# Row statistics and router logits made per segment inside the recurrent chain, instead of in one pass over x in the first step

## The chip, the core and the metric

The kernel runs on one core of a Trainium2 chip. A core has a matrix engine (TensorE, PE in the profile; its weight loads are listed as PEld), a vector engine (VectorE, DVE), an activation engine (ScalarE, ACT), GpSimd (POOL) and SyncE (SP), which here only issues DMAs. Each engine runs its own instructions in order and waits on semaphores for the others. SP, POOL and ACT all issue DMAs, and 16 DMA engines of the core carry them out. SBUF holds working data; PSUM holds what PE writes.

The metric is the device time of one execution in microseconds, lower is better. A run is one such execution; the profile is of one more.

## The reference

Two results are added to x. A is a recurrent transformer layer with memory: x is normalised per row and cut into 64 segments of 32 rows; each segment attends with 8 memory rows in front, and the first 8 output rows become the next segment's memory. B picks the two rows with the largest router logit and runs an expert MLP on them alone.

```python
x = A_x                                   # 1 x 2048 x 1024, bf16
xn = _layernorm(x, axis=-1)
return x + _A_ref(xn, A_mem0, A_Wq, A_Wk, A_Wv, A_Wo, A_seg_len) + _B_ref(xn, B_w_r, ...)

# A, for each segment s of 64, H = 32 heads of 128:
h = jnp.concatenate([mem, xs], axis=1)    # 8 + 32 rows
q, k, v = h @ Wq, h @ Wk, h @ Wv
o = softmax(mask(q k^T * scale)) v @ Wo
mem = o[:, :M, :]                         # the next segment needs it
outs.append(o[:, M:, :])

# B
r = x @ w_r                               # one logit per row, of the normalised x
idx = jnp.argsort(-r, axis=-1)[:, :2]
y = silu(x_sel @ w_gate) * (x_sel @ w_up) @ w_down * sigmoid(r_sel)
return x + scatter of y to the two rows
```

Each row's mean and variance are needed before its segment is projected; all 2048 logits are needed before B can choose.

## The kernel before

**Steps.** The loop over s (64 steps) is the chain: step s needs the memory that step s - 1 made. A step's main rows are the first 24 of its segment, together with the 8 memory rows, so that PE works on 32 rows. The 8 rows left over of each segment (columns of the output that no memory depends on) are collected for four segments, again 32 rows, a group G = s // 4 with j = s % 4; their projections ("passes") are spread over the four steps, in PE's gaps. The leftover rows of group G + 1 are loaded in the step with j = 0 (`get_left`, tile BX) and projected to q, k and v over the steps of group G. Those of the group that has just ended are loaded once more for the residual (tile OL, at w = 11 of the step with j = 3), and their output is finished in the next step with j = 0 (`copy_unit` of unit "o").

**Order inside a step.** Six phases p = 0 to 5 (q, k for heads 0 to 15; q, k for heads 16 to 31; v for both), each over eight weight granules kc = 0 to 7 of 128 x 2048; then the output projection over w = 0 to 15. For each granule PE runs four matmuls side by side into PSm (L835). All else is placed by hand: `hook(p, kc, fn)` puts the instructions of `fn` into every engine's order right after granule kc of phase p. What stands in a hook is in program order on its engine, so a matmul there holds up every later matmul until its inputs are ready. The order at j = 0 before: `sum_left` of the old group at (2, 3), `get_left` at (1, 1), `scores(0)` at (2, 6), `load_seg` of the next step's X at (2, 4), `scores(1)` at (4, 6), `norm_left` at (5, 3). After phase 5 come `norm_seg` of the next step, `attend(1, ...)` at w = 5 and w = 8 (there the normalised rows XN are transposed too), and at the end OB, the step's output, whose memory rows are transposed into the next ST (`mem_to_st`). `transposes` of a phase stand at granule 3 of the next one; the first of them in a step also transposes LX, the leftover q and k (`turn_lx`, into PTB2).

**Weights.** 64 granules of 512 KB: 44 are resident in SBUF after step 0 (`load_resident`), 20 are streamed (`fetch`), 19 of them in every later step, through five buffers (tile g) on SP's queue; one is kept in PSUM. `fetch` issues the next transfer when PE has finished with a buffer. Step 0 loads everything and copies the streamed granules into a compact place in DRAM (`copy_block`, tile wsc).

**Statistics and router before.** In step 0 all of x is read in eight 512 KB transfers (`load_x`, tile XP, into homes that resident weights take later). `side` hangs on the granules of step 0: `row_stats` of each of 16 row tiles, `spread` (selection matmuls that move the means and deviations to the partitions where the steps want them, kept in PSUM as MR, ML and MLR), `router_tile` (normalise, multiply with the broadcast router weights WRB, sum), then `router_out` and `router_top`, which finds the two rows. MISC, XR, XP lie in homes of resident weights, whose loads wait for them. Later steps only read two numbers per row (`two_rows`).

**Tail.** After step 63 the last group's leftover rows are finished, the two routed rows are gathered (L931), and the MLP weights (tile MW), which SP has been fetching into the homes that the last step frees, are multiplied as they land.

Of the kernel before, what the change touches and what calls it, by code (L numbers as in the profile page):

```python
# [8 lines left out]
BF16 = mybir.dt.bfloat16  # L9
# [42 lines left out]
def kernel(  # L52
# [96 lines left out]

    IDENT = const.tile([P, P], BF16, name="IDENT")  # L150
# [22 lines left out]
    nc.vector.memset(NMSK, 0.0)  # L173

    hm = resident[-1]
    MISC = home(hm, [P, 2048], BF16, "MISC")
    SELM = MISC[:, 0:512].rearrange("p (s g r) -> p s g r", s=4, g=4)
    SELL = MISC[:, 512:640].rearrange("p (g s r) -> p g s r", g=4, s=4)
    MV = MISC[:, 640:672].rearrange("p (t c) -> p t c", c=2)
    VE = MISC[:, 672:688]  # L180
    RB = MISC[:, 688:704]
    S6 = MISC[:, 704:704 + 24].bitcast(F32).rearrange("p (c s) -> p c s", c=2)
    RI16 = MISC[:, 728:792].bitcast(F32).rearrange("p (t c) -> p t c", c=2)
    RF = MISC[:, 792:824].bitcast(F32)
    MF = MISC[:, 824:824 + 2 * (XM + 1)].bitcast(F32)
    SELR = MISC[:, 888:888 + 128].rearrange("p (g r s) -> p g r s", g=4, r=XL)
    WRB = MISC[:, 1024:2048]
# [41 lines left out]
    def spread(t0, t1):  # L229

        n = t1 - t0
        sd_rows(MV[:, t0:t1, :], VE[:, t0:t1])
        PD = BT[:, 256:448]
        for s in range(6):
            if s < 4:
                sel = SELM[:, s, :, :].rearrange("p g r -> p (g r)")
            else:
                sel = SELL.rearrange("p g s r -> p (g s r)") if s == 4 else SELR.rearrange("p g r s -> p (g r s)")
# [798 lines left out]
```

## Time and profile before

| | |
|---|---|
| median of 3 runs | 1864.08 us (1862.82 to 1864.24) |
| the profiled execution | 1863.48 us, its span 1861.8 us, mean PE clock 0.961 |
| busy: PE, DVE, ACT, POOL | 1559.9 us (84%), 958.3 (51%), 726.8 (39%), 456.0 (24%) |
| moved by DMA | 712.04 MB, mean 382 GB/s, 671.18 MB of it on SP's queue |
| end of step 0, of step 62, of step 63 | 133.4 us, 1776.7 us, 1803.1 us (starts of L908) |

How to read it: the page is of one execution. Busy times are unions of an engine's instructions; a matmul's end is modelled, so that a busy PE is not PE at its peak, and four matmuls side by side count once. The share of DMA is the mean busy share of the 16 engines and can pass 1 slightly, because packets overlap. The GB/s of the 40 slices lie between 357 and 406, but for the last one at 338. In rows of groups stand, after the bar, the busy time and the mean length of one instruction, and then the idle time of the engine before them with what ended it. In rows of a timeline stand start, length, engine, line, operation, tiles and, in brackets, the idle time before the row. Times to landing are counted from a DMA's issue to its semaphore.

### The profile page before, as it was taken

Reading aid. Unit: us, or ns where it says so; the run is one execution under the profiler, and the core shown is the slowest. Engines: PE = TensorE matmul, PEld = TensorE weight load, DVE = VectorE, ACT = ScalarE, POOL = GpSimd, SP = SyncE. Lnnn points to the kernel's source line nnn. Section 1 sums busy time; section 2 is a strip of 40 time slices with the busy share of each in tenths; the row PEclk is TensorE's granted clock in tenths of the full one; section 3 lists DMA queues with packets and bytes.
Section 4 is the critical chain, followed back from the end, with each engine's and each line's share of the span. In section 5 each row is a group of like instructions: output and inputs, shape, how many; then the busy total and the mean of one; then the engine's idle time right before and its main releaser. Section 6 shows DMA issues by size and latency. Waiting matters only on the chain.

```text
span 1861.8 us, 76772 instructions
## 1 busy us (share of the span) xinstructions
PE 1559.9 (84%) x32930; PEld 791.5 (43%) x32930; DVE 958.3 (51%) x3015; ACT 726.8 (39%) x2124; POOL 456.0 (24%) x898
## 2 busy tenths in 40 slices
PE   3458899888889988888988889988888988988864
PEld 1124444444444444444444444444444444444433
DVE  6825455544555455455545555555544554555540
ACT  1114444444344444344444444444444443444430
POOL 3111321213131322323132221323132122312220
PEclk9669999999999999999999999999999999999985
DMA  9999999999999999999999999999999999999998
GB/s 357 391 367 370 373 393 388 389 380 386 381 384 387 385 391 375 363 394 368 398 383 383 388 394 398 384 397 376 383 377 374 381 383 383 385 393 374 398 406 338
DMA packets 230310, 712.04 MB, mean 382 GB/s; under 512 B 39040, under 2 KB 52912, under 8 KB 229968
## 3 DMA queue, kind: packets, MB, share of 16 engines
q1 hardware_dynamic: 192592, 671.18, 93.3%
q0 software_dynamic: 28736, 28.08, 4.7%
q10 hardware_dynamic: 8640, 7.87, 1.2%
q8 instruction: 258, 4.23, 0.8%
q14 instruction: 84, 0.69, 0.1%
HBM read 694.32 MB, written 22.29 MB: 385 GB/s over the span
## 4 chain that ended last, share of the span: by engine, by line
DMA 60%; PE 32%; DVE 4%; issue 1%; ACT 1%; SPq 1%; POOL 0%; ACTq 0%; DVEq 0%; POOLq 0%
DMA g<-wsc 52%; PE PSm L835 17%; PE PSl L583 4%; PE BT L667 2%; PE WO L592 2%; PE WO L596 2%; DMA XP<-in_A_x_dram 2%; PE WL L616 1%; DMA MW<-in_B_w_gate_dram 1%; DMA g<-in_A_Wq_dram 1%; DVE XR L257 1%; DMA MW<-in_B_w_up_dram 1%; DMA wres<-in_A_Wo_dram 1%; DMA g<-in_A_Wo_dram 1%; DMA g<-in_B_w_down_dram 1%
## 5 line engine op out<-in xcount | busy, mean ns | idle before, releaser
L835 PE MATMUL PSm<-wres,ST 128*32 128x512 bf16 x8448 | 696.7, 382 | 6.1 <-DMA wres<-in_A_Wv_dram 3.9
L835 PEld LDWEIGHTS <-ST 128*32 128x32 bf16 x12288 | 323.6, 96 | 415.7 <-issue 171.4
L835 PE MATMUL PSm<-g,ST 128*32 128x512 bf16 x3588 | 358.4, 385 | 102.2 <-DMA g<-wsc 77.6
L854 ACT CAST XB<-PSm 128x512 bf16<-128x512 f32 x256 | 150.8, 589 | 268.3 <-PE PSm L835 265.8
L499 POOL DMA_DIRECT2D LX<-ql_d x63 | 35.3, 560 | 813.3 <-PE WO L596 375.0
L682 DVE COPY KT<-BT 128x512 bf16<-128x512 bf16 x112 | 45.9, 410 | 281.6 <-PE BT L667 280.6
L583 PE MATMUL PSl<-wres,STL 128*32 128x512 bf16 x2112 | 184.7, 391 | 0.1
L910 POOL DMA_DIRECT2D out_dram<-X x256 | 129.9, 515 | 212.4 <-DVE X L908 164.8
L285 POOL DMA_DIRECT2D X<-in_A_x_dram x256 | 130.0, 514 | 174.0 <-PE PSm L835 69.1
L393 ACT COPY BK<-KEPT 128x512 bf16<-128x512 bf16 x189 | 109.2, 614 | 119.7 <-DMA ql_d<-XBl 65.6
L596 PEld LDWEIGHTS <-OT 128*32 128x32 bf16 x4096 | 105.6, 97 | 93.1 <-issue 71.5
L592 PE MATMUL WO<-wres,OT 128*32 128x512 bf16 x1536 | 124.8, 387 | 10.3 <-DMA wres<-in_A_Wo_dram 9.2
L675 ACT COPY QT<-BT 128x512 bf16<-128x512 bf16 x128 | 75.0, 586 | 134.3 <-PE BT L506 85.0
L596 PE MATMUL WO<-g,OT 128*32 128x256 bf16 x1536 | 78.4, 280 | 57.5 <-DMA g<-wsc 49.1
L754 PEld LDWEIGHTS <-VM 32*128 32x128 bf16 x2048 | 65.7, 91 | 110.7 <-issue 90.3
L667 PE MATMUL BT<-IDENT,XB 128*128 128x128 bf16 x1024 | 102.0, 222 | 9.4 <-ACT XB L854 8.0
L667 PEld LDWEIGHTS <-XB 128*128 128x128 bf16 x1024 | 58.5, 98 | 117.9 <-ACT XB L854 69.7
L596 PE MATMUL WO<-wres,OT 128*32 128x256 bf16 x2560 | 107.2, 277 | 0.0
L583 PEld LDWEIGHTS <-STL 128*32 128x32 bf16 x3072 | 83.7, 98 | 51.0 <-issue 7.2
L864 ACT CAST VM<-PSm 128x512 bf16<-128x512 f32 x128 | 76.6, 598 | 71.0 <-PE PSm L835 70.6
L397 DVE COPY g<-KEPT 128x512 bf16<-128x512 bf16 x126 | 47.6, 420 | 98.2 <-PE PSm L835 47.1
L699 DVE TENSOR_TENSOR BS<-BS,CT 128x96 f32<-128x96 f32 (+1 forms) x256 | 59.1, 231 | 73.0 <-PE BS L692 68.5
(180 smaller groups left out, 2587.1 us busy)
## 6 DMA issues: line engine op xcount, KB each, us to landing
g<-wsc SPq DMA_DIRECT2D x1134, 512.0 KB, 6.1
g<-wsc SPq DMA_DIRECT2D x63, 256.0 KB, 5.8
LX<-ql_d POOLq DMA_DIRECT2D x63, 128.0 KB, 5.6
ql_d<-XBl ACTq DMA_DIRECT2D x60, 128.0 KB, 5.8
MW<-in_B_w_gate_dram SPq DMA_DIRECT2D x16, 448.0 KB, 9.7
MW<-in_B_w_up_dram SPq DMA_DIRECT2D x16, 448.0 KB, 9.0
wres<-in_A_Wk_dram SPq DMA_DIRECT2D x12, 512.0 KB, 11.1
MW<-in_B_w_down_dram SPq DMA_DIRECT2D x12, 512.0 KB, 9.7
```

The costliest lines, as they stand in the source:

```text
L285: nc.gpsimd.dma_start(out=X[s % 2][32 * g:32 * g + XM, :], in_=x2[s * SEG:s * SEG + XM, 256 * block(g):256 * (block(g) + 1)])
L393: copy(out=back[c][:, :], in_=KEPT_COLS[KEPT_WHOLE][c])
L583: nc.tensor.matmul(PSl[32 * jq:32 * jq + 32, :], lhsT=STL[:, g % KC, :], rhs=part(Gv, jq), start=first_, stop=last_, tile_position=(0, 32 ...
L592: nc.tensor.matmul(PS[r0:r0 + 32, :], lhsT=lhs(h), rhs=Gv[:, D * hs + 512 * c:D * hs + 512 * (c + 1)], start=(w == 0), stop=(w == N_WIDE - ...
L596: nc.tensor.matmul(PS[32 * g:32 * g + 32, 0:256], lhsT=lhs(h), rhs=Gv[:, D * hs + 256 * block(g):D * hs + 256 * (block(g) + 1)], start=(w ...
L667: nc.tensor.transpose(out=PTq[:, il, :, :].rearrange("p j r -> p (j r)"), in_=XB[:, il * P:(il + 1) * P], identity=IDENT[:, :])
L675: nc.scalar.copy(out=QT[half][:, :, :], in_=pv)
L754: nc.tensor.matmul(o, lhsT=VM[half][q0:q0 + 32, il * P:(il + 1) * P], rhs=PTm[q0:q0 + 32, il, 0:NK], start=True, stop=False, tile_position ...
L835: nc.tensor.matmul(PSm[32 * jq:32 * jq + 32, :], lhsT=ST[:, 2 * block(kc // 2) + kc % 2, :], rhs=part(Gv, jq), start=(kc == 0), stop=(kc = ...
L854: nc.scalar.copy(out=XB[:, :], in_=PSm[:, :])
L864: nc.scalar.copy(out=VM[half][:, :], in_=PSm[:, :])
L910: nc.gpsimd.dma_start(out=out2[s * SEG:s * SEG + XM, 256 * block(g):256 * (block(g) + 1)], in_=OB[32 * g:32 * g + XM, :])
```

## The change

The pass over x in step 0, its transfers, its buffers and the selection matmuls are dropped. Instead each step computes the statistics of the next step's rows where they lie, on 128 partitions that hold four quarters of 32 rows: `part_stats` makes mean and mean square of each quarter on DVE and splits them into two bf16 parts, `sum_stats` adds the four quarters with two matmuls against S4 (four identity blocks), `spread_of` makes the variance, `root_of` makes its inverse root as exp(-0.5 ln v) on ACT. X of the next step, BX of the next group and OL of the old group each go through this. Router logits are eight one-column matmuls per step from the transposed rows (`logits`, and `logits_left` per group); they gather in PSUM until step 63, where `router_out` and `router_in` take them through DRAM, and `router_top` runs behind the last step. The table set with exp and ln is named at the start; constants move to PSUM columns.

```diff
+    nc.scalar.preload_act_table_set("natural_log_exp_and_others")
...
-    MR = BS[:, 320:320 + 2 * NSEG].rearrange("p (s c) -> p s c", c=2)
-    ML = BS[:, 448:448 + 2 * NT].rearrange("p (t c) -> p t c", c=2)
-    MLR = BS[:, 480:480 + 2 * NT].rearrange("p (t c) -> p t c", c=2)
+    LOGIT = BS[0:XM, 320:320 + NSEG]
+    LOGITL = BS[0:32, 384:384 + NT]
...
+    S6 = BS[:, 412:418]
+    SUMS, SUMSL = BT[:, 510:512], BT[:, 508:510]
...
+    def part_stats(x):
+        t = stats[0] = one.tile([P, 8], F32, tag="nm", name="AV")
+        av, hl = t[:, 0:2], t[:, 4:6].bitcast(BF16)
+        nc.vector.bn_stats(out=S6, in_=x)
+        nc.vector.bn_aggr(out=av, in_=S6)
+        nc.vector.scalar_tensor_tensor(out=av[:, 1:2], in0=av[:, 0:1], scalar=av[:, 0:1], in1=av[:, 1:2],
+                                       op0=ALU.mult, op1=ALU.add)
+        nc.vector.tensor_scalar(out=hl[:, 0:2], in0=av, scalar1=0.25, scalar2=None, op0=ALU.mult)
+        nc.vector.scalar_tensor_tensor(out=hl[:, 2:4], in0=av, scalar=0.25, in1=hl[:, 0:2], op0=ALU.mult, op1=ALU.subtract)
+
+    def sum_stats(sums):
+        hl = stats[0][:, 4:6].bitcast(BF16)
+        for c in range(2):
+            nc.tensor.matmul(sums, lhsT=S4[:, :], rhs=hl[:, 2 * c:2 * c + 2], start=(c == 0), stop=(c == 1),
+                             skip_group_check=True)
+
+    def spread_of(sums):
+
+        var = VAR if sums is SUMS else VARL
+        nc.vector.tensor_scalar(out=var, in0=sums[:, 0:1], scalar1=sums[:, 0:1], scalar2=sums[:, 1:2],
+                                op0=ALU.mult, op1=ALU.subtract)
+        nc.vector.tensor_scalar(out=var, in0=var, scalar1=0.0, scalar2=1e-5, op0=ALU.min, op1=ALU.subtract)
+
+    def root_of(rst):
+        nc.scalar.activation(out=rst, in_=VAR if rst is RST else VARL, func=ACTF.Ln, scale=-1.0)
+        nc.scalar.activation(out=rst, in_=rst, func=ACTF.Exp, scale=-0.5)
...
+    def logits(st, s):
+        for kc in range(KC):
+            nc.tensor.matmul(LOGIT[:, s:s + 1], lhsT=st[:, 2 * block(kc // 2) + kc % 2, 0:XM], rhs=WRT[:, kc:kc + 1],
+                             start=(kc == 0), stop=(kc == KC - 1), skip_group_check=True)
...
+    def router_in():
+        rrow[0] = home(1, [1, S], BF16, "RROW")
+        nc.gpsimd.dma_start(out=rrow[0][:, :], in_=r_d[:, :])
...
+    def sum_left(t):
+
+        ab, m, r = AB, SUMSL[:, 0:1], RSTL
+        nc.vector.tensor_scalar(out=ab[:, 1:2], in0=m, scalar1=r, scalar2=-1.0, op0=ALU.mult, op1=ALU.mult)
...
-    load_x(0)
-    nc.sync.dma_start(out=WRB, in_=B_w_r.unsqueeze(0).to_broadcast([P, D]))
-    load_seg(0)
+    load_seg(0, nc.scalar)
+    WR8 = one.tile([P, 512], BF16, tag="vl1", name="WR8")[0:KC, 0:P]
+    nc.scalar.dma_start(out=WR8, in_=B_w_r.rearrange("(k p) -> k p", p=P))
...
-            if g in side:
-                side[g]()
...
-            if n_x_left and g % 2 == 1:
-                load_x(n_x_left.pop(0))
-            while todo_res and todo_res[0] <= g + 2 * 64 // n_str + 8 and (todo_res[0] < resident[-10] or g >= 2 * NT + 12):
+            while todo_res and todo_res[0] <= g + 2 * 64 // n_str + 8:
                 load_resident(todo_res.pop(0))
...
-            if g in resident:
+            if g in resident and g > 1:
                 free_homes.append(g)
...
         if j == 0 and s > 0:
-            hook(2, 3, lambda: sum_left(xl_of[0], G - 1))
-        hook(*((1, 0) if s > 0 else (2, 3)), clear_pl)
+            hook(0, 3, lambda: part_stats(xl_of[0]))
+            hook(1, 0, lambda: sum_stats(SUMSL))
+            hook(1, 1, lambda: spread_of(SUMSL))
+            hook(1, 1, lambda: root_of(RSTL))
+            hook(1, 2, lambda: sum_left(xl_of[0]))
...
+        if j == 0 and G + 1 < NT:
+            a = 5 if s == 0 else 2
+            hook(1 if s > 0 else 4, 0 if s > 0 else 1, get_left)
+            hook(a, 1 if s == 0 else 5, lambda: part_stats(nxt["xl"]))
+            hook(a, 2 if s == 0 else 6, lambda: sum_stats(SUMSL))
+        hook(*((1, 0) if s > 0 else (2, 3)), clear_pl)
...
         if j == 0 and G + 1 < NT:
-            hook(4 if s == 0 else 1, 1, get_left)
-            hook(5, 3, lambda: norm_left(nxt["xl"], G + 1))
+            hook(*((5, 3) if s == 0 else (2, 7)), lambda: spread_of(SUMSL))
+            hook(*((5, 3) if s == 0 else (4, 1)), lambda: root_of(RSTL))
+            hook(5, 3, lambda: norm_left(nxt["xl"]))
+        if s + 1 < NSEG:
+            hook(4, 5, lambda: part_stats(X[(s + 1) % 2][:, :]))
+            hook(4, 6, lambda: sum_stats(SUMS))
         hook(4, 6, lambda: scores(1))
         hook(5, 0, exponent)
+        if s + 1 < NSEG:
+            hook(4, 7, lambda: spread_of(SUMS))
+        else:
+            hook(0, 5, router_out)
+            hook(1, 6, router_in)
...
         if s + 1 < NSEG:
+            root_of(RST)
             xn = norm_seg(s + 1)
...
+        if s + 1 < NSEG:
+            logits(nxt["st"], s + 1)
+            if left_too is not None:
+                logits_left(STL, G + 1)
         run_passes(7, 0)
...
-    sum_left(xl_of[0], NT - 1)
+    part_stats(xl_of[0])
+    sum_stats(SUMSL)
+    spread_of(SUMSL)
+    root_of(RSTL)
+    sum_left(xl_of[0])
     copy_unit("o", NSEG - 1, "vector")
+    router_top()
```

More of the change, by code (lines that the diff above doesn't have):

```diff
@@ L172 @@
         nc.vector.memset(X[b][:, :], 0.0)
[L173 to L187, printed above, removed]
+    nc.vector.memset(T3, 0.0)
+    S4 = const.tile([P, P], BF16, name="S4")
+    for q in range(0, P, 32):
+        nc.vector.tensor_copy(out=S4[q:q + 32, :].rearrange("p (h c) -> p h c", h=4),
+                              in_=IDENT[q:q + 32, q:q + 32].unsqueeze(1).to_broadcast([32, 4, 32]))
+    MF = one.tile([P, 512], BF16, tag="bC", name="MF")[:, 0:2 * (XM + 1)].bitcast(F32)
     nc.vector.memset(MF, 0.0)
-    nc.vector.memset(MISC[:, 0:640], 0.0)
     for q0 in range(0, P, 32):
@@ new lines, in logits_left @@
+    def logits_left(stl, G):
+        for kc in range(KC):
+            nc.tensor.matmul(LOGITL[:, G:G + 1], lhsT=stl[:, kc, :], rhs=WRT[:, kc:kc + 1],
+                             start=(kc == 0), stop=(kc == KC - 1), skip_group_check=True)
+    def router_out():
+        RW = home(0, [P, 2048], BF16, "RW")
+        RB, RBL, RT, RTL = RW[0:XM, 0:NSEG], RW[0:32, 64:64 + NT], RW[0:NSEG, 128:128 + XM], RW[0:NT, 160:192]
+        nc.vector.tensor_copy(out=RB, in_=LOGIT)
+        nc.vector.tensor_copy(out=RBL, in_=LOGITL)
+        nc.tensor.transpose(out=PTB[0:NSEG, 0:XM], in_=RB, identity=IDENT[0:XM, 0:XM])
+        nc.tensor.transpose(out=PTB[0:NT, 32:64], in_=RBL, identity=IDENT[0:32, 0:32])
+        nc.vector.tensor_copy(out=RT, in_=PTB[0:NSEG, 0:XM])
+        nc.vector.tensor_copy(out=RTL.rearrange("p (s r) -> p r s", s=4), in_=PTB[0:NT, 32:64].rearrange("p (r s) -> p r s", s=4))
+        nc.gpsimd.dma_start(out=r_d[0].rearrange("(s r) -> s r", r=SEG)[:, 0:XM], in_=RT)
+        nc.gpsimd.dma_start(out=r_d[0].rearrange("(t s r) -> t s r", s=4, r=SEG)[:, :, XM:SEG],
+                            in_=RTL.rearrange("p (s r) -> p s r", s=4))
@@ L280, in block @@
+    rrow = [None]
+    top = []
+    def router_in():
+        rrow[0] = home(1, [1, S], BF16, "RROW")
+        nc.gpsimd.dma_start(out=rrow[0][:, :], in_=r_d[:, :])
+    def router_top():
+        VI = one.tile([P, 256], F32, tag="bE", name="VI")[0:1, 0:16]
+        top.extend([VI[:, 0:8], VI[:, 8:16].bitcast(U32)])
+        V8, I8 = top
+        nc.vector.max(out=V8[:, :], in_=rrow[0][:, :])
+        nc.vector.max_index(out=I8[:, :], in_max=V8[:, :], in_values=rrow[0][:, :])
     def block(g):
@@ L492, in after @@
                 fetch_moe()
-    n_x_left = list(range(n_x, NT // 2))
     def new_lx(s):
@@ L873 @@
         if s + 1 < NSEG:
+            root_of(RST)
             xn = norm_seg(s + 1)
@@ L917 @@
             ST = nxt["st"]
-    sum_left(xl_of[0], NT - 1)
+    part_stats(xl_of[0])
+    sum_stats(SUMSL)
+    spread_of(SUMSL)
+    root_of(RSTL)
+    sum_left(xl_of[0])
     copy_unit("o", NSEG - 1, "vector")
+    router_top()
+    V8, I8 = top
     free_homes += [-1] * N_SLOT
```

129 lines of the change are left out of this document (33 added, 96 removed).

## The prediction

> **What bounds the kernel now.** I read the page first, then the busy time by stretches, then what TensorE (PE) waits for.
>
> ```profile
> span 1861.8 us, 76772 instructions
> DMA  9999999999999999999999999999999999999998
> DMA 60%; PE 32%; DVE 4%; issue 1%; ACT 1%; SPq 1%; POOL 0%; ACTq 0%; DVEq 0%; POOLq 0%
> ```
>
> The DMA row is nine tenths or more in every slice but the last, and the chain that ended last is mostly transfers. The stretches say the same in numbers (columns: busy time and count for PE, weight load, DVE, ACT, POOL, then PE clock, DMA share, GB/s):
>
> ```profile
> 10.00:40.00 30.00, 17.04 (x178) 7.74 (x179) 19.55 (x46) 3.45 (x8) 4.20 (x8) 0.89 1.04 405
> 100.00:140.00 40.00, 18.35 (x266) 8.23 (x262) 11.13 (x27) 6.35 (x23) 4.39 (x9) 0.62 0.95 359
> 140.00:1780.00 1640.00, 1455.12 (x31097) 737.02 (x31097) 860.23 (x2749) 693.67 (x2040) 415.01 (x811) 1.00 1.01 384
> ```
>
> The first two lie in step 0, which fills the weights; the third is steps 1 to 62, 26.5 us each (1640/62). The DMA engines are full in all of it, and PE is behind them by little: 1455 of 1640 us busy. What PE waits for, from 140 to 1780 us (total, times, longest):
>
> ```profile
> PE PSm L835 <- DMA g<-wsc: 76.3, 155, 2.0
> PE WO L596 <- DMA g<-wsc: 49.1, 100, 1.2
> PE WO L592 <- DMA g<-wsc: 23.6, 52, 2.1
> ```
>
> 149 us in all, or 2.4 us per step, is all the room that PE has. So **bytes set the time, but only as long as PE gives the five stream buffers back in time**. How much lateness the buffers forgive is read from one transfer (columns of the last line: least, median, most):
>
> ```profile
> L370 SPq DMA_DIRECT2D g<-wsc x1197: 319/320/2648, 121.5 to 1795.0; - x200
> ...
> DMA to landing us min/median/max: 3.2/6.1/21.0
> ```
>
> A granule usually lands 6.1 us after its issue and can land after 3.2; the 2.9 us between is time queued behind earlier granules. If PE hands buffers back later than that, the queue runs dry. The 3.2 may belong to a 256 KB granule. A full one carries 262 KB more, 0.7 us at 384 GB/s, so the spare is 2.2 to 2.9 us. I take 2.4.
>
> **The change, part by part.**
>
> *Removed transfers.*
>
> ```profile
> XP<-in_A_x_dram SPq DMA_DIRECT2D x8, 512.0 KB, 10.7
> MISC<-in_B_w_r_dram SPq DMA_DIRECT2D x1, 256.0 KB
> ```
>
> 8 x 524288 + 262144 bytes are 4.46 MB, in step 0, where the DMA is full: 11.0 us at 405 GB/s, 12.4 us at 359. **Minus 11.4 us** at some 390, between the two. The DVE work on x there (16 x L222, L255, L257) goes too; it lay beside full DMA engines and gives nothing of its own. The next limit of step 0 is the same queue: PE was busy 18 of 40 us in its last stretch. The first loads of X and the router weights, five small DMAs, move to ACT's queue, and POOL is four DMAs sooner at the other start-up loads; the large loads already run behind them, so an earlier first matmul gives nothing.
>
> *Added statistics.* Each use of `part_stats` is five DVE instructions, then two tiny matmuls of `sum_stats`, before anything behind them on PE may run. Nearest rows (count, then busy us and mean ns):
>
> ```profile
> L222 DVE BATCH_NORM_STATS2 MISC<-XP 128x6 f32<-128x512 bf16 x32 | 20.5, 683 | 4.9 <-DMA XP<-in_A_x_dram 4.5
> L223 DVE BATCH_NORM_AGGREGATE MISC<-MISC 128x2 bf16<-128x12 f32 x16 | 3.3, 209 | 0.6
> L350 DVE TENSOR_SCALAR RI<-RI 128x1 f32<-128x1 f32 x16 | 2.5, 154 | 0.5
> L239 PE MATMUL BT<-MISC 128*128 128x2 bf16 (+1 forms) x12 | 0.6, 177 | 7.2 <-ACT MISC L227 7.2
> ```
>
> Half of 683 ns for 256 columns, 209, and three at 154: 1.01 us, with handovers 1.1 us on DVE; the matmuls start 50 ns apart (0.6/12), 0.1 us. **So 1.2 us from the moment its input is there**, and PE, which runs in order, stands still for as much of it as it arrives early. DVE holds two waits, for a landing and for its own earlier work; everything after them on DVE waits too, and PE waits for DVE.
>
> *Where the wait is longest.* In every fourth step (4, 8, ..., 60; 15 steps, "opening steps" here) statistics of OL, the previous group's leftover rows, stand at phase 0 granule 3, their sum at phase 1 granule 0. OL's load is not moved. Step 56, POOL and PE (start, length):
>
> ```profile
> 1591.52 2.37 POOL L337 DMA_DIRECT2D OL<-in_A_x_dram  x4
> ```
>
> ```profile
> 1597.37 0.40 PE L835 MATMUL PSm<-wres,ST 128*32 128x512 bf16 x4
> 1598.43 0.40 PE L835 MATMUL PSm<-g,ST 128*32 128x512 bf16 x4 [0.66 <-DMA g<-wsc]
> ...
> 1599.65 0.39 PE L506 MATMUL BT<-IDENT,LX 128*128 128x128 bf16 x4
> ```
>
> ```profile
> L337 POOL DMA_DIRECT2D OL<-in_A_x_dram x64: 578/590/637, 213.0 to 1781.3; - x64
> ...
> DMA to landing us min/median/max: 4.5/5.9/7.3
> ```
>
> The fourth issue starts at 1591.52 + 2.37 - 0.59 = 1593.3 and lands 5.9 later, 1599.2. Plus 1.2 is 1600.4. The row at 1597.37 is phase 1 granule 0; the next granule ran at 1598.43. Before, OL was needed by DVE alone, at phase 2. Now PE waits 2.0 us beyond its old wait; changing the array's shape there and back adds 0.1: **2.1 us**. Behind it, `turn_lx` at granule 3 overwrites the PSUM columns that `sum_left` reads; sums, two DVE, two ACT and one DVE operation at 0.15 to 0.2 us each, and the handovers, make 1.4 us, against 1.2 us of PE work (1598.43 to L506 at 1599.65): **0.2 us**.
>
> *The same step, twice more.* BX is summed at phase 2 granule 6 ahead of `scores(0)`, which PE reaches just after its KT copy on DVE: the full **1.2 us**. X of the next step is summed ahead of `scores(1)`:
>
> ```profile
> 1609.54 0.45 DVE L738 STREAM_TRANSPOSE PT<-BX 128x256 bf16<-128x256 bf16 x1
> ```
>
> ```profile
> 1609.29 0.21 PE L690 MATMUL BS<-KT,QT 128*32 128x40 bf16 x4 [0.23 <-DVE BX L733]
> ```
>
> DVE ends the softmax of half 0 only at 1609.99, 0.7 us after PE was there; then 1.2: **1.9 us**. An opening step thus falls 2.1 + 0.2 + 1.2 + 1.9 = 5.4 us behind; I let 0.4 us be won back from small waits between: 5.0. Less the 2.4 us spare, the transfers stand idle **2.6 us per opening step, 39 us for 15**. From below: 4.5 behind, 2.9 spare, 24 us; from above: nothing won back, 0.4 of logits added, 2.2 spare, 54 us.
>
> *Other steps.* One sum, of X:
>
> ```profile
> 1627.47 2.01 POOL L285 DMA_DIRECT2D X<-in_A_x_dram  x4 [3.48 <-DMA out_dram<-X]
> 1634.63 0.42 DVE L682 COPY KT<-BT 128x512 bf16<-128x512 bf16 x1 [0.36 <-PE BT L667]
> ```
>
> ```profile
> 1635.32 0.19 PE L690 MATMUL BS<-KT,QT 128*32 128x40 bf16 x4
> ```
>
> ```profile
> L285 POOL DMA_DIRECT2D X<-in_A_x_dram x256: 505/505/871, 3.8 to 1759.6; - x128
> ...
> DMA to landing us min/median/max: 3.9/5.1/11.9
> ```
>
> X lands near 1627.5 + 1.5 + 5.1 = 1634.1, the copy ends at 1635.05, and 1.2 later is 1636.25: PE loses 1.0 us. That is under the 2.2 us spare and under the 2.4 us of waits per step, so it hides. X landing some microseconds later in a few steps breaks that: from 0 to 12 us, **I take 3**.
>
> *Logits.* Eight one-column matmuls per step, 16 in opening ones; nearest, by spacing:
>
> ```profile
> L983 PE MATMUL GU<-T,MW 128*128 128x2 bf16 x448 | 12.6, 165 | 7.6 <-issue 7.6
> ```
>
> 12.6/448 is 28 ns: 0.2 us and about as much for the shape change, at the step's end, where PE waits for granules anyway. Without that cover 0.4 x 63 = 25 us of PE work. The two ACT operations of `root_of` stand ahead of XN, which the transposes at w = 8 need (step 33):
>
> ```profile
> L227 ACT ACTIVATE MISC<-MISC 128x1 bf16<-128x1 bf16 (+1 forms) x2 | 0.4, 213 | 15.5 <-DVE MISC L226 15.5
> ```
>
> ```profile
> 1005.77 0.34 DVE L296 TENSOR_SCALAR XN<-X,RI 128x256 bf16<-128x256 bf16 x1
> ...
> 1007.79 0.28 PE L305 MATMUL BT<-IDENT,XN 128*128 128x128 bf16 x2
> ```
>
> 0.4 us against 1.7 us of room: nothing. POOL keeps its queue order but for BX's loads, which go ahead of a memset.
>
> *Tail.* `router_top` moves behind the last step, with about 1.06 + 0.3 + 0.5 + 0.5 us of statistics ahead of it.
>
> ```profile
> L270 DVE MAX8 CT<-RROW 1x8 f32<-1x2048 bf16 x1 | 2.3, 2283 | 6.0 <-DMA RROW<-r_d 6.0
> L271 DVE FIND_INDEX8 CT<-CT,RROW 1x8 uint32<-1x2048 bf16 x1 | 2.3, 2273 | 0.0
> ```
>
> ```profile
> 1820.24 4.19 PE L983 MATMUL GU<-T,MW 128*128 128x2 bf16 x151
> ...
> 1839.14 1.25 PE L983 MATMUL GU<-T,MW 128*128 128x2 bf16 x41 [2.92 <-issue]
> ```
>
> About 7 us of new DVE work, of which some 4 lay beside POOL's stores of OL: the expert matmuls would start 3 us later, at 1823.2, and 12.6 us of them end at 1835.8, before the last weights let them end at 1840.4. **Nothing**, with 4.6 us of cover left; beyond that, all of it. The router's row goes through DRAM in step 63 instead of step 0, three small DMAs on POOL with over 20 us to land, and takes homes 0 and 1 from the expert weights: 42 homes and five buffers still hold 46 tiles.
>
> **Sum:** -11.4 + 39 + 3 = +30.6 us on 1863.5, the profiled execution's own time (span 1861.8 and 1.7 around it): 1894.1. The median of the runs is 0.6 above that execution, within their spread; I say **1894 us**.
>
> By the Trainium skill, page "DMA: Bandwidth & Descriptors", section on the anatomy of one DMA, about 2.0 us of a transfer is fixed, most of it the completion. With 1.4 us for the granule's own bytes that would leave 2.7 of the 6.1 us as spare, and the sum would be 1890.
>
> **Rivals.**
>
> 1. *The buffers forgive it all.* The five buffers hold seven microseconds of transfers, and PE's waits of 2.4 us per step vanish as it falls behind. For it: full DMA slices everywhere. Against it: 5.0 us of lateness in one step exceeds both. Then only bytes count: 1863.5 - 11.4 = 1852, **faster**. It decides for faster if the loss per opening step is under 0.5 us. Chance 0.17.
> 2. *Half forgiven*: only OL's wait outlasts the spare, by about 0.8 us, 15 x 0.8 = 12 against 11.4: about 1864, no change. Chance 0.08.
> 3. *The tables are exchanged.* `root_of` uses Ln and Exp in each step; if they lay in different table sets, ACT would load twice per step.
>
> ```profile
> L227 ACT ACT_TABLE_LOAD x2 | 2.6, 1283 | 0.9 <-PEq L1018 0.9
> ```
>
>    2 x 1.28 us per step, before XN with its 1.7 us, of which 0.4 are taken: 1.3 us late with the rest, 20 us more over the opening steps, 1914. Chance 0.07. The Trainium skill, "ScalarE: Activation LUTs", "What ACT_TABLE_LOAD costs", gives about 2.66 us for a switch with its drain, which would make it (5.3 - 1.3) x 15 = 60 us, 1954; its section on table sets puts ln and exp in one set, which the change names, and speaks against this rival. No run here shows it yet.
> 4. *The waits chain into the following steps*, or more of the late X landings count: over 1925. Chance 0.06.
>
> My forecast has 0.62, by itself 1876 to 1918. **Range 1852 to 1925** takes in rivals 1 to 3. About 0.2% (3.7 us) is what a measurement of this kernel can tell from no change: faster 0.17, same 0.08, slower 0.75.
>
> **What would show it.** Right: XP gone and step 0 shorter by 11 us; PE waiting at the first small matmul of the opening steps for DVE, 2 us or more, and DVE there for OL; opening steps longer by 2.6 us, the others alike; DMA share under 1 in them alone. Wrong: opening steps as long as before (rival 1), ACT_TABLE_LOAD in every step (rival 3), or all steps longer by the same amount (then PE's own added work counts, and not one late load).

## The result, and the profile after

The kernel became slower, and ten times as much as forecast: 2185.79 us median (2180.23 to 2193.19, 4 runs) against 1863.45 (1861.18 to 1864.24, 4 runs), a ratio of 1.1735, 95% interval [1.1688, 1.1781]. The direction was right; the 322 us lie far outside the range. The profiled execution took 2193.19 us. From its page: the span, the clock and DMA rows of the 40 slices, and the chain that ended last.

```profile
span 2191.5 us, 79074 instructions
PEclk8589998989888899899889989898999989998895
DMA  9999898989989898898979889898988989898998
DMA 30%; PE 30%; DVE 20%; issue 10%; ACT 6%; POOL 4%; ACTq 0%; DVEq 0%; POOLq 0%; SPq 0%
PE PSm L835 9%; DMA g<-wsc 8%; DMA X<-in_A_x_dram 7%; PE WO L576 5%; DMA OL<-in_A_x_dram 4%; DMA out_dram<-X 3%; PE PSl L563 3%; PE WO L572 3%; DVE BS L198 2%; POOL X L276 2%; PE BT L647 2%; DMA wres<-in_A_Wk_dram 1%; PE BT L208 1%; DVE DN L694 1%; DVE PT L701 1%
```

Transfers had 60% of the chain and DVE 4%; now DVE has 20%, and the loads of X and OL, 12 and 16 KB each, stand on it. The stretch of 140 to 1780 us in busy times (columns as in the prediction), with the same stretch of before quoted there at clock 1.00, DMA share 1.01 and 384 GB/s:

```profile
140.00:1780.00 1640.00, 1306.79 (x26368) 662.80 (x26365) 836.49 (x2655) 595.23 (x1834) 349.75 (x679) 0.92 0.90 317
```

Where the time sits along the run is read from the X add that ends each step, first and last of 64 starts. Before, then after:

```profile
L908 DVE TENSOR_TENSOR X<-WO,SUM x64: 424/425/427, 133.4 to 1803.1; 128x256 bf16<-128x256 f32 x64
```

```profile
L909 DVE TENSOR_TENSOR X<-WO,SUM x64: 424/425/426, 118.4 to 2133.7; 128x256 bf16<-128x256 f32 x64
```

Step 0 is 15.0 us shorter, steps 1 to 63 are 345.6 us longer (2015.3 against 1669.7), and the tail is as long as it was (57.8 us of the span behind the last start, before 58.7). The 64 starts also give the mean length of a step by j, each from one profiled execution; the later kernels of the experiments stand beside it:

| us per step, steps 2 to 62 | j = 0 (opening) | j = 1 | j = 2 | j = 3 |
|---|---|---|---|---|
| before | 27.4 | 26.1 | 26.5 | 26.0 |
| after | 39.3 | 30.3 | 29.5 | 29.1 |
| small values in SBUF (e2) | 34.8 | 27.5 | 27.5 | 27.8 |
| sums moved too (e5) | 29.8 | 26.7 | 26.7 | 26.9 |
| BX's sum moved again (e7) | 27.9 | 26.6 | 27.2 | 26.7 |
| e7 without the statistics (e9) | 27.3 | 26.8 | 27.0 | 26.4 |

So the opening steps lost 11.9 us each, and every other step 3 to 4 us, where the prediction had 3 us for all of them together. What PE waited for, from 140 to 2120 us (total, times, longest):

```profile
PE BT L208 <- DVE AV L202: 154.5, 90, 5.9
PE BS L734 <- DVE X L288: 109.0, 62, 2.9
PE BT L734 <- DVE BX L331: 46.8, 14, 4.0
PE PSm L835 <- DMA g<-wsc: 42.9, 58, 2.1
PE BT L647 <- DVE BS L214: 14.3, 14, 1.0
PE BT L734 <- DVE BS L214: 12.0, 27, 0.9
```

The first is the sums, which the prediction priced. The second comes 62 times, once in every step: `attend(1, 0)` waits for the last instruction of `norm_seg`. The third, fifth and sixth are of the same kind: attention or a transpose waits until DVE has read a number. Step 33, an ordinary one, shows the order of events (start, length, engine, line):

```profile
1163.28 0.43 DVE L198 BATCH_NORM_STATS2 BS<-X 128x6 f32<-128x256 bf16 x1 [0.67 <-DMA X<-in_A_x_dram]
...
1164.45 0.36 PE L208 MATMUL BT<-AV,S 128*128 128x2 bf16 x2 [1.75 <-DVE AV L202]
...
1166.63 0.50 DVE L685 TENSOR_TENSOR BS<-BS,NM 128x320 f32<-128x320 f32 x1
...
1167.49 0.17 DVE L216 TENSOR_SCALAR BS<-BS 128x1 f32<-128x1 f32 x1
1167.69 0.42 ACT L689 ACTIVATE BS<-BS 128x320 f32<-128x320 f32 x1 [1.38 <-DVE BS L216]
...
1171.47 0.16 ACT L220 ACTIVATE BS<-BS 128x1 f32<-128x1 f32 x1
1171.66 0.23 DVE L283 TENSOR_SCALAR BS<-BS 128x1 f32<-128x1 f32 x1 [0.78 <-ACT BS L220]
...
1172.79 0.35 DVE L288 TENSOR_SCALAR X<-X,BS 128x256 bf16<-128x256 bf16 x1
1173.29 0.17 PE L734 MATMUL BS<-PT,VM 32*128 32x40 bf16 x1 [1.75 <-DVE X L288]
```

The statistics take 1.17 us from the landing of X to the sum, as forecast. The exponent (L689) has its own input at 1167.13, when L685 ends, and starts 0.56 us later, behind `spread_of` (L216); of the 1.38 us in its brackets only this last part is due to L216. The two share nothing but the PSUM tile BS: VAR is column 403 of it, the scores are columns 0 to 319. And `attend(1, 0)`, which writes columns 0 to 159 of BS, has its own inputs by 1170.98 (in the trace the softmax's transposed result is done at 1170.30, the values at 1170.98) and waits until 1173.29 for L288, which reads AB in columns 406 and 407. By the Trainium skill, page "PSUM — Partial Sum Buffer", section "PSUM bank collisions raise a hardware error", two engines may not touch one bank in the same partitions at once, whatever the columns, and PSUM is to be guarded by bank, not by address. BS and BT have the size that the page gives for one bank, and the waits in this trace are what such a guard looks like. Each of the two tiles fills one bank, so no run here tells a guard by bank from a guard by tile.

### The profile page after: what moved, and what is told of

Read it like the earlier page. It is cut to its first block, busy times and chain, and to the rows that moved or that the text cites. A ratio compares the mean times of both kernels' runs of the same rounds, so it can differ in the third digit from the quotient of the medians.

```text
span 2191.5 us, 79074 instructions
## 1 busy us (share of the span) xinstructions
PE 1687.6 (77%) x33752; PEld 857.3 (39%) x33752; DVE 1061.3 (48%) x3368; ACT 753.1 (34%) x2313; POOL 455.5 (21%) x895
## 4 chain that ended last, share of the span: by engine, by line
DMA 30%; PE 30%; DVE 20%; issue 10%; ACT 6%; POOL 4%; ACTq 0%; DVEq 0%; POOLq 0%; SPq 0%
PE PSm L835 9%; DMA g<-wsc 8%; DMA X<-in_A_x_dram 7%; PE WO L576 5%; DMA OL<-in_A_x_dram 4%; DMA out_dram<-X 3%; PE PSl L563 3%; PE WO L572 3%; DVE BS L198 2%; POOL X L276 2%; PE BT L647 2%; DMA wres<-in_A_Wk_dram 1%; PE BT L208 1%; DVE DN L694 1%; DVE PT L701 1%
## 5 line engine op out<-in xcount | busy, mean ns | idle before, releaser
L835 PE MATMUL PSm<-wres,ST 128*32 128x512 bf16 x8448 | 729.4, 397 | 21.8 <-DMA wres<-in_A_Wv_dram 13.5
L835 PE MATMUL PSm<-g,ST 128*32 128x512 bf16 x3588 | 377.7, 403 | 54.2 <-DMA g<-wsc 44.0
L563 PE MATMUL PSl<-wres,STL 128*32 128x512 bf16 x2112 | 190.5, 396 | 0.7 <-issue 0.3
L734 PEld LDWEIGHTS <-VM 32*128 32x128 bf16 x2048 | 72.9, 94 | 243.4 <-issue 236.4
L208 PE MATMUL BT<-AV,S 128*128 128x2 bf16 x192 | 31.3, 164 | 173.7 <-DVE AV L202 170.9
L572 PE MATMUL WO<-wres,OT 128*32 128x512 bf16 x1536 | 142.5, 441 | 2.8
L734 PE MATMUL BT<-PT,VM 32*128 32x40 bf16 x1024 | 90.1, 182 | 59.5 <-DVE BX L331 46.8
L576 PEld LDWEIGHTS <-OT 128*32 128x32 bf16 x4096 | 118.3, 112 | 40.4 <-issue 10.5
L734 PE MATMUL BS<-PT,VM 32*128 32x40 bf16 x512 | 45.1, 182 | 109.0 <-DVE X L288 109.0
L576 PE MATMUL WO<-wres,OT 128*32 128x256 bf16 x2560 | 127.4, 320 | 0.3 <-issue 0.3
L647 PE MATMUL BT<-IDENT,XB 128*128 128x128 bf16 x1024 | 104.9, 227 | 24.6 <-DVE BS L214 14.3
```

The source lines that it names most:

```text
L563: nc.tensor.matmul(PSl[32 * jq:32 * jq + 32, :], lhsT=STL[:, g % KC, :], rhs=part(Gv, jq), start=first_, stop=last_, tile_position=(0, 32 ...
L572: nc.tensor.matmul(PS[r0:r0 + 32, :], lhsT=lhs(h), rhs=Gv[:, D * hs + 512 * c:D * hs + 512 * (c + 1)], start=(w == 0), stop=(w == N_WIDE - ...
L576: nc.tensor.matmul(PS[32 * g:32 * g + 32, 0:256], lhsT=lhs(h), rhs=Gv[:, D * hs + 256 * block(g):D * hs + 256 * (block(g) + 1)], start=(w ...
L647: nc.tensor.transpose(out=PTq[:, il, :, :].rearrange("p j r -> p (j r)"), in_=XB[:, il * P:(il + 1) * P], identity=IDENT[:, :])
L734: nc.tensor.matmul(o, lhsT=VM[half][q0:q0 + 32, il * P:(il + 1) * P], rhs=PTm[q0:q0 + 32, il, 0:NK], start=True, stop=False, tile_position ...
L835: nc.tensor.matmul(PSm[32 * jq:32 * jq + 32, :], lhsT=ST[:, 2 * block(kc // 2) + kc % 2, :], rhs=part(Gv, jq), start=(kc == 0), stop=(kc = ...
```

## The experiments

Three theories: **S**, PE waits for the sums; **B**, PE waits because the small values were moved into the banks that attention writes; **C**, each wait is paid again in TensorE's clock. The medians of before on the chips of these runs lay between 1863.5 and 1868.8, so single runs are read to some 10 us.

### e1: no statistics inside the steps

```diff
-            hook(0, 3, lambda: part_stats(xl_of[0]))
-            hook(1, 0, lambda: sum_stats(SUMSL))
...
-            hook(4, 5, lambda: part_stats(X[(s + 1) % 2][:, :]))
-            hook(4, 6, lambda: sum_stats(SUMS))
...
-            root_of(RST)
             xn = norm_seg(s + 1)
```

> The changed kernel without its statistics inside the steps: part_stats, sum_stats, spread_of and root_of run only ahead of step 0, and every later step reuses those values (the output is another one). Logits, normalisations and the dropped pass over x stay. Theory S (the statistics are the whole cost, by the waits that they bring PE): the excess of 322 us goes, and what is left is the kernel before less the removed transfers, about 1852, at most 1890 if the values read from PSUM by norm_seg still hold up attend(1). Rival L (the logits, the tail or the loads moved to other queues carry a good part): above 1900.

Measured: 1914.57 us (one run; before 1867.95 on this chip). 271 of the 322 us go, so the statistics and their waits are most of it. The time is above theory S's 1890 and in the range of rival L, but PE's new waits are neither for logits nor for loads in other queues; 140 to 1850 us:

```profile
PE PSm L821 <- DMA g<-wsc: 79.6, 164, 1.8
PE BT L734 <- DVE BX L331: 44.0, 14, 3.5
...
PE BS L734 <- DVE X L288: 11.1, 15, 1.2
```

`norm_left` reads its mean in BT and its root in BS and stands on DVE behind the softmax; `attend(0, 0)` writes BT and still waits 44 us for it, with no statistics anywhere near. That is B without S. The wait for L288, 109.0 us in the changed kernel, is down to 11.1 although AB still lies in BS: it takes the shared bank and the late statistics together.

### e2: the small values in SBUF

```diff
+    CV = const.tile([P, 16], F32, name="CV")
-    VAR, VARL, RST, RSTL, AB = BS[:, 403:404], BS[:, 408:409], BS[:, 404:405], BS[:, 405:406], BS[:, 406:408]
+    VAR, VARL, RST, RSTL, AB = CV[:, 3:4], CV[:, 4:5], CV[:, 5:6], CV[:, 6:7], CV[:, 7:9]
+    MEAN, MEANL = CV[:, 9:10], CV[:, 10:11]
...
+        nc.vector.tensor_copy(out=MEAN if sums is SUMS else MEANL, in_=sums[:, 0:1])
```

> The changed kernel with its small values (VAR, VARL, RST, RSTL, AB, the masks and a copy of the means) in an SBUF tile instead of columns of the PSUM tiles BS and BT; room for it comes from a summing matrix of 32 columns, so each sum is 8 matmuls of 32 columns instead of 2 of 128. Order unchanged. Theory B (the values lie in the PSUM banks that attention writes, so its matmuls wait until DVE and ACT have read them): the four PE waits for X L288, BX L331 and BS L214, 109.0 + 46.8 + 14.3 + 12.0 = 182 us, go nearly whole, and with them some of the lost clock: 1990, between 1950 and 2040. Rival Q (PE waits there because the DVE queue is late anyway, whichever memory holds the values): the waits move to the next consumer, above 2130.

Measured: 2028.98 us (one run; before 1867.95), **157 us less** than the changed kernel, within theory B's range; Q falls. PE's waits, 140 to 1850 us (this run's chain goes on to 1970; up to there the first line is 135.1 us, 90 times):

```profile
PE BT L210 <- DVE AV L203: 128.0, 86, 4.6
...
PE BT L737 <- DVE CV L218: 14.1, 32, 0.8
PE BT L650 <- DVE CV L218: 13.1, 14, 0.9
```

The waits for X and BX are gone (the summing matrix of 32 columns, which came with this edit, stands in e6 too, where the values stay in PSUM and the waits remain); what is left of B is `spread_of` reading the sums, which PE has to write into some bank. The sums now lead.

### e3: OL loaded earlier

```diff
-            if w == 11 and j == 3:
+            if w == 0 and j == 3:
```

> The changed kernel with the load of OL issued at granule 0 of the output projection instead of granule 11, nothing else moved. Theory O (in the opening steps PE waits for OL's landing, 4.1 us each): that wait goes, 15 x 4.1 = 62 us, and some clock with it: 2110, between 2090 and 2135. Rival D (DVE is late there by its own earlier work, or POOL's queue holds the load back all the same): 2170 or more.

Measured: 2146.15 us (one run; before 1867.95): 40 us less, where 51 to 96 were expected. PE's waits, 140 to 2080 us:

```profile
PE BS L734 <- DVE X L288: 110.7, 62, 2.9
PE BT L208 <- DVE AV L202: 109.2, 75, 4.8
```

The waits at the sums fell by 45 us and not by 62: of the three in an opening step, OL's went from 4.1 us to nothing, but PE now comes sooner to BX's, which rose from 0.6 us to about 2. A new wait took part of the place of the old one.

### e4: the kernel before without seven of the eight loads of x

```diff
-        return XP[t // 2][:, (t % 2) * D:(t % 2 + 1) * D]
+        return XP[0][:, (t % 2) * D:(t % 2 + 1) * D]
-        if g % 2 == 1 and n_x < NT // 2:
+        if g % 2 == 1 and n_x < 1:
-    n_x_left = list(range(n_x, NT // 2))
+    n_x_left = []
```

> The kernel before with only the first of its eight loads of x in step 0 (the statistics and the router read that one again and again; the output is another one): 3.67 MB fewer. Theory T (step 0 is bound by bytes, 11.4 us for 4.46 MB): 9.4 us faster, 1854, between 1851 and 1857. Rival N (the transfers are hidden beside the loads of weights): 1863. If step 0 loses more than bytes by other queueing, as its 15 us in the changed kernel hint: 1850 or less.

Measured: 1854.05 us (10 runs) against 1867.95, ratio 0.9932 [0.9907, 0.9957]: 12.7 us faster, by the interval 8 to 17. Bytes (9.4 us) are within it. In its profiled execution step 0 ends at 123.5 us:

```profile
L908 DVE TENSOR_TENSOR X<-WO,SUM x64: 424/425/427, 123.5 to 1801.8; 128x256 bf16<-128x256 f32 x64
```

The four kernels with all loads of x (before, d1 to d3) end it at 129.4 to 133.4 us, the nine without any (the changed one and e1 to e9 except e4) at 117.4 to 121.5. The two means, 131.9 and 120.1, are 11.8 us apart: bytes, with nothing besides that shows. The steps behind step 0 are the same program as before and their means by j differ by -0.1 to +0.2 us, a scatter to reckon with wherever such means are compared.

### e5 and e7: the same statistics, placed where PE need not wait

On top of e2; part_stats also works in an SBUF tile of its own.

```diff
-            if w == 11 and j == 3:
+            if w == 0 and j == 3:
-            hook(a, 1 if s == 0 else 5, lambda: part_stats(nxt["xl"]))
-            hook(a, 2 if s == 0 else 6, lambda: sum_stats(SUMSL))
+            hook(2, 6, lambda: part_stats(nxt["xl"]))
+            hook(3, 1, lambda: sum_stats(SUMSL))
...
+            if w == 1 and s + 1 < NSEG:
+                sum_stats(SUMS)
+                spread_of(SUMS)
+                root_of(RST)
+                xn = norm_seg(s + 1)
```

> All the statistics kept, but no longer where PE has to wait for them: small values in SBUF as in the second experiment, OL loaded at granule 0 of the output projection, BX's part_stats behind the DVE work of scores(0) and its sum two granules into phase 3, X's part_stats behind the DVE work of scores(1), and its sum, spread, root and norm_seg at granule 1 of the output projection. Theory B plus S (what costs is where PE waits, not the work of the statistics): PE waits for transfers alone again, and the time is that of the kernel before less its transfers, 1852, between 1846 and 1872. Rival V (DVE, ACT and PE have no room for the added work itself, 25 or more instructions a step): the softmax comes late instead, 1890 or more.

Measured: 1928.31 us (1912.88 to 1931.33, 5 runs) against 1868.78, ratio 1.034 [1.027, 1.0409]. Another 101 us gone, but not the 1846 to 1872 of theory B plus S; the number lies in rival V's range. The trace shows another cause than a late softmax. PE's waits, 140 to 1850 us:

```profile
PE BT L211 <- DVE AV L204: 32.7, 14, 2.5
```

One sum of an opening step, BX's, still stops PE for 2.3 us. e7 moves it and its spread from (3, 1) to (3, 4):

> The fifth kernel with one thing more: BX's sum and spread three granules later, at phase 3 granule 4 ahead of the exponent. In the fifth kernel's trace PE still waits 32.7 us there (14 times, 2.3 us each) and the DMA engines are idle 6 per cent of the opening steps. Theory S (a wait of PE that empties the stream buffers counts): the opening steps become 2.0 to 2.3 us shorter, the kernel 30 to 35 us faster than the fifth, 1880 to 1897 on the same chip. Rival H (the softmax of half 0 or the transposes behind it are late instead): under 10 us.

Measured: 1888.67 us (1883.46 to 1890.27, 4 runs) against 1867.63, ratio 1.0103 [1.0063, 1.0142]: 40 us less than e5 by the medians and 25 by the two profiled executions, where theory S had 30 to 35. The opening steps went from 29.8 to 27.9 us. BX's sum does not come free even so; 140 to 1820 us:

```profile
PE BT L211 <- DVE AV L204: 14.5, 15, 1.0
```

### e6: the waits filled, so that the clock stays up

```diff
+    def add_zeros(PS, Gv, n):
+        for i in range(n):
+            for jq in range(4):
+                nc.tensor.matmul(PS[32 * jq:32 * jq + 32, :], lhsT=ZERO[:, :], rhs=Gv[:, 512 * jq:512 * (jq + 1)],
+                                 start=False, stop=False, tile_position=(0, 32 * jq), skip_group_check=True)
+    FILL_ALL = {(4, 6): 2}
+    FILL = {(1, 0): 14, (4, 6): 6, (5, 4): 10}
...
+                    add_zeros(WO, res_tiles[0], 5)
                 attend(1, 0)
```

What it is about, from the changed kernel, step 33, stretch by stretch (the stretch and its length; busy time and count of PE, PEld, DVE, ACT and POOL; PE clock, DMA share, GB/s):

```profile
1159.00:1162.50 3.50, 3.50 (x63) 1.56 (x60) 2.85 (x9) 1.80 (x4) 0.00 (x0) 1.00 1.03 378
1162.50:1164.50 2.00, 0.25 (x5) 0.14 (x2) 1.19 (x6) 0.00 (x0) 0.00 (x0) 1.00 1.02 401
1164.50:1168.00 3.50, 3.47 (x66) 1.53 (x65) 2.28 (x8) 0.89 (x2) 0.00 (x0) 0.54 0.94 342
1168.00:1171.40 3.40, 3.29 (x76) 1.34 (x68) 2.62 (x7) 1.95 (x11) 0.00 (x0) 0.97 0.95 269
1171.40:1173.30 1.90, 0.15 (x5) 0.04 (x3) 1.24 (x4) 0.19 (x2) 0.00 (x0) 1.00 0.65 207
1173.30:1175.20 1.90, 1.90 (x58) 1.14 (x62) 0.76 (x3) 0.80 (x6) 0.00 (x0) 0.96 0.88 349
1175.20:1178.40 3.20, 3.20 (x71) 2.51 (x67) 1.32 (x4) 1.47 (x5) 0.55 (x1) 0.50 1.05 399
```

PE is all but idle in the second and the fifth stretch, under 2 us each, and each is followed, at once or 2 us later, by some 3.4 us at half the clock.

> The changed kernel with PE kept busy during part of its waits: matmuls with a matrix of zeros that add nothing to a sum that is open anyway, ahead of the waiting instruction: 3.0 us of them ahead of OL's sum, 1.3 ahead of X's in the opening steps and 0.4 in the others, 2.2 ahead of attend(0,0) in the opening steps, 1.1 ahead of attend(1,0) (at 0.215 us for four; the summing matrix has 32 columns, to make room for the zeros). The order and every wait on DVE stay. Theory C (a wait of about 2 us or more is paid twice: TensorE's granted clock falls to 0.5 for 3.4 us or a multiple of it behind it, 334 us of the changed kernel's trace are such time): low-clock time falls below 100 us and the time to 2060, between 2030 and 2100. Rival W (the slow stretches lie beside other waits and cost nothing of their own): 2170 to 2200.

Measured: 2169.38 us (one run; before 1868.78): 16 us less, not 126. The clock did stay up; the changed kernel from 150 to 2130 us, and this one from 150 to 2110 us:

```profile
150.00:2130.00 1980.00, 1578.73 (x31872) 799.77 (x31864) 1007.50 (x3196) 718.84 (x2215) 418.14 (x813) 0.92 0.90 318
```

```profile
150.00:2110.00 1960.00, 1688.95 (x35814) 881.50 (x35807) 1009.04 (x3199) 715.90 (x2216) 416.39 (x811) 0.98 0.91 322
```

Time at the lower clock fell from 334 to 92 us in the clock's own records. So theory C is right about the clock and wrong about its price. A reading that fits the stretches above, though no run shows it by itself: the slow stretch behind one wait ends in the next wait, whose end DVE sets, and PE that is faster in between waits longer there. PE's waits, 140 to 2120 us:

```profile
PE BT L210 <- DVE AV L203: 71.6, 89, 3.2
...
PE BS L744 <- DVE X L290: 54.8, 51, 1.6
PE BT L744 <- DVE BX L333: 26.1, 14, 1.9
PE BT L657 <- DVE BS L216: 14.3, 14, 1.0
PE BT L744 <- DVE BS L216: 12.8, 28, 0.9
```

These five were 336.6 us in the changed kernel and are 179.6 here, 157 less, for 183 us of zeros (15 x 7.5 + 47 x 1.5). If the other 26 us cost their full length, the clock is worth 16 + 26 = 42 us; if they cost nothing, 16.

### e8: no logits

```diff
-            logits(nxt["st"], s + 1)
-            if left_too is not None:
-                logits_left(STL, G + 1)
```

> The seventh kernel without the router logits of steps 1 to 63 (they stay zero; the output is another one). Theory P (the logits lie where PE waits for granules anyway): the same time as the seventh kernel, within 6 us. Rival L (the column matmuls and the change of the array's shape are PE's own work that the transfers wait for): 0.4 us a step, 25 us faster than the seventh.

Measured: 1896.10 us (1887.51 to 1898.83, 4 runs), ratio 1.0138 [1.0092, 1.0183], beside e7's 1.0103 on the same chip: 7 us more by the medians, a little outside theory P's 6, with intervals that overlap. There is no gain, let alone the 25 us of rival L: the logits cost nothing that shows.

### d1, d2, d3: how much of PE's lateness is forgiven

The kernel before, with `add_zeros` as a pure delay of PE and nothing else.

```diff
+    DELAY, DELAY_OPEN = {(4, 6): 5}, {(4, 6): 5}
...
+                    add_zeros(PSm, res_tiles[0], (DELAY_OPEN if j == 0 else DELAY).get((p, kc), 0))
```

> The kernel before with a delay of PE alone: in each of steps 1 to 62, ahead of the work behind phase 4 granule 6 (where the changed kernel sums X), five times four matmuls with zeros that add nothing, 5 x 0.215 = 1.08 us. It is the 1.0 us that the prediction had in the ordinary steps. Theory G (PE has 2.4 us of waits for granules per step, and what fits in them is free): no change, 0 to 5 us. Rival F (the buffers forgive nothing, each microsecond of PE counts): 67 us slower.

> The same with 10 more ahead of attend(1,0) in the output projection: 3.23 us per step at the two places where the changed kernel's ordinary steps wait longest. Theory G: 3.23 less the 2.4 us of waits, 0.8 us per step, 50 us slower, between 30 and 75. If transfers and PE overlap less well near the bound, up to 100. Rival F: 200 us. If it is below 30, the buffers forgive more than PE's waits.

> The kernel before with 5.4 us of such zeros in the opening steps alone (2.15 at phase 1 granule 0, 1.3 at phase 2 granule 6, 1.9 at phase 4 granule 6), the lateness that the prediction had there. By the prediction's spare of 2.4 us: 15 x 2.6 to 3.0, 39 to 45 us slower. If only PE's own waits of those steps, 3.1 us for granules, are forgiven: 15 x 2.3 = 35. If the following steps make it up: 0 to 15. If nothing is forgiven: 81.

| | zeros in all | measured | per us |
|---|---|---|---|
| d1: 1.08 us in every step | 67 us | 1902.81 (4 runs), ratio 1.0213 [1.0149, 1.0277]: +39 | 0.6 |
| d2: 3.23 us in every step | 200 us | 1984.79 (one run): +121 | 0.6 |
| d3: 5.4 us in opening steps | 81 us | 1926.53 (4 runs), ratio 1.0326 [1.0261, 1.0391]: +63 | 0.8 |

(before 1863.67 on this chip.) Neither G nor F: over all steps there is no threshold of 2.4 us. The first microsecond costs 0.6 (0.4 to 0.8 by the interval), and so does the mean of three. PE still waits for granules with 3.23 us of zeros in each step; d2, 140 to 1900 us:

```profile
PE PSm L844 <- DMA g<-wsc: 93.1, 131, 2.2
```

and the stretch of 140 to 1780 us, d1 and then d2:

```profile
140.00:1780.00 1640.00, 1488.78 (x31794) 764.39 (x31790) 846.90 (x2703) 678.52 (x2005) 406.56 (x792) 1.00 1.00 377
```

```profile
140.00:1780.00 1640.00, 1516.76 (x32435) 787.34 (x32431) 805.12 (x2563) 642.98 (x1896) 385.89 (x752) 1.00 0.98 357
```

The DMA engines look as full as before (share 1.00 and 0.98) and move 377 and 357 GB/s where they moved 384.

The price is not paid evenly. By the starts of the X add, mean us per step beyond before, one profiled execution each:

| | j = 0 (opening) | j = 1 | j = 2 | j = 3 |
|---|---|---|---|---|
| d1 | 0.2 | 0.6 | 0.6 | 0.7 |
| d2 | 0.7 | 2.3 | 1.6 | 3.3 |
| d3 | 2.8 | 0.8 | 0.3 | 0.4 |

The opening steps themselves forgive 0.9 us of 1.08, 2.5 of 3.23 and 2.6 of 5.4, close to the prediction's 2.4; but d3's other steps, which have no delay of their own, pay some 1.5 us of it back. The ordinary steps have no such room: 1.08 us costs them 0.6.

### e9: e7 without the statistics

> The seventh kernel without the statistics inside the steps (as in the first experiment; the output is another one): what its last 20 us over the kernel before and 33 over 1856 come from. Theory M (the statistics' instructions themselves, some 20 on DVE, PE and ACT in a step, still cost about 0.5 us a step): 1852 to 1860. Rival R (something else in the change, which no experiment has touched): 1880 or more.

Measured: 1871.85 us (10 runs) against 1863.67, ratio 1.0036 [1.0003, 1.0068]. The time lies between the two theories. About 13 us (1.0103 less 1.0036, of 1866; the intervals just overlap) go with the statistics, but not as theory M had it, as half a microsecond of instructions in each step: by the table in the result section the opening steps are some 0.7 us shorter than e7's and the others differ by -0.3 to +0.2. What goes is mainly e7's last wait, 1.0 us at BX's sum in each opening step. About 20 us over 1852 are something that no run here isolates. They lie in the ordinary steps (0.4 to 0.7 us longer than before, where e4, with the same steps as before, has up to 0.2) and not in the opening ones. It is not the logits (e8); the order of the loads and the new places of tiles in SBUF are what is left. That stays open.

## Why the prediction went wrong, point by point

- **What bounds.** "bytes set the time, but only as long as PE gives the five stream buffers back in time" holds; the room of 2.4 us per step in PE's waits does not, and the spare of 2.4 us in the buffers holds only for the opening step itself (d3: 2.6 of 5.4 us), part of which the following steps pay back. A load is issued when PE releases its buffer, so a late PE makes the next granule late, and PE's waits for granules are not a stock that is used up first. The runs with a pure delay put a price of 0.6 to 0.8 us on each, from the first. This is the step that made ordinary steps cost nothing: 1.08 us in every step, the 1.0 that was to hide, cost 39 us in d1. The 2.0 us of fixed time that the prediction takes from the Trainium skill stand there in a section on DMAs that GpSimd issues, while the granules go out on SP's queue; no run here shows them.
- **Removed transfers, -11.4 us.** Right: step 0 is 11.8 us shorter by the means over all kernels (see e4); the 15.0 of the one pair of profiles has scatter in it.
- **1.2 us from input to sum.** Right: 1.17 us in step 33.
- **Waits at the sums in an opening step.** X 1.9, measured 2.0; BX 1.2, measured 0.6; OL 2.1, measured 4.1. For OL I took one DMA's median landing of 5.9 us; four have to land, and `bn_stats` began 5.6 to 8.3 us behind the fourth issue. PE also came sooner, since its waits for granules in front had gone. In the other steps X was to cost 1.0 and cost 1.0 to 1.5 by the means of j.
- **`root_of` "0.4 us against 1.7 us of room: nothing".** This is **the step that failed first**. It was priced against XN and its transpose at w = 8. The instruction of PE that really came next was `attend(1, 0)` at w = 5, which has no data in common with it, only the bank of BS. `norm_left` against `attend(0, 0)` and `spread_of` against the exponent and the transposes are the same omission. The text of the changed kernel has AB, RST and VAR as columns of BS; the trace of before even had the case in small, ahead of `attend(1, ...)`, where RI was copied out of BS:

```profile
L754 PE MATMUL BS<-PT,VM 32*128 32x40 bf16 x512 | 44.5, 178 | 2.8 <-DVE RI L277 2.6
```

  In the changed kernel these waits are 182 us together (109.0 + 46.8 + 14.3 + 12.0), where the prediction had nothing; moving the values out of the banks took 157 us off the time.
- **Logits, tail.** Right: no gain without the logits, and the tail kept its length.
- **Exchanged tables (rival 3).** Fell: the whole run has four table loads, one at the start and three in the tail, none in a step. The Trainium skill, "ScalarE: Activation LUTs", section "Table sets: the hidden batching unit", puts ln and exp in one set; the trace agrees.

```profile
L150 ACT ACT_TABLE_LOAD x1 | 1.3, 1283 | 0.9 <-PEq L1029 0.9
L231 ACT ACT_TABLE_LOAD x1 | 1.3, 1283 | 0.0
L962 ACT ACT_TABLE_LOAD x1 | 1.3, 1283 | 0.0
L997 ACT ACT_TABLE_LOAD x1 | 1.3, 1283 | 0.0
```

- **Rivals 1, 2 and 4.** The buffers forgave neither all nor half. Rival 4, over 1925, came true in its number, but mainly by another way than it named: a wait of its own in each step. The chaining that it named is there, but small: some 1.5 us in the three steps behind each opening one in d3, 22 us in all.
- **The direction.** Slower was right, and does not hang on the banks: without them (e2) the kernel is still 161 us slower than before, mainly by the sums that the prediction priced. Moving the sums was worth some 141 us (e2 to e7), where it had 42 for all of their waits.
- **What would show it.** The last sign named, all steps longer, is what came, though not by the same amount; the guess beside it, that PE's own added work would then count, was wrong.

The account of the 322 us, by medians across chips and so to some 10 us each: shared banks 157 (changed kernel to e2), OL's, X's and part of BX's sums 101 (to e5), most of the rest of BX's 40 (to e7), what is left of the statistics 13 to 17 (to e9), not isolated about 20, less the 11 to 13 us of removed transfers. The order of the experiments decides how the first two are shared out, since the wait ahead of `attend(1, 0)` goes either with the statistics (e1) or with the shared bank (e2). The clock's 16 to 42 us lie inside the first three. No version that does the whole computation beats the kernel before; e7, with the same computation as the changed kernel, is 1.0% slower than it.

## What to carry to other kernels

Price a moved value against the next instruction that touches its bank or stands behind it in a queue, not only against the one that reads it; a scalar parked in a bank that PE writes in every step ties PE to whoever reads it last. Where PE itself releases the stream buffers, its waits for granules are not free time: a few matmuls that add zero, put in as a pure delay, show in one run what a microsecond of PE costs. When one wait is removed, look which wait PE reaches next before the gain is booked in full.

## What was not expected of the hardware

- **Short waits cost clock.** Of the changed kernel's gaps between matmuls at full clock, counted over the trace from 140 to 2120 us, 1 of 33 of 1.0 to 1.5 us, 16 of 46 of 1.5 to 2.0 us, all 6 of 2.0 to 2.5 us and 38 of 45 longer ones were followed within 2 us by a granted clock of 0.5; most such stretches last 3.41 us or two or three times that. The Trainium skill, page "TensorE: Matmul & The Clock Gate", section "What's actually happening", has the free-running window of about 3.4 us, and the lengths agree; its rule to keep idle gaps under some 3.4 us (section "HAM oscillation — how this bites in real kernels") does not hold here: gaps of 1.5 to 2.5 us were enough in 22 of 52 cases.
- **A full DMA row is not a rate.** 384, 377 and 357 GB/s show as shares of 1.01, 1.00 and 0.98.
